# A memset that signals the change of rows, and a maximum at the start of the next step, in an attention and gated dense kernel

## The chip, the cores and the metric

One NeuronCore of one Trainium2 chip runs the whole kernel. The metric is the time of one execution on the device in microseconds (us); smaller is better. A profiled execution gives, beside its time, a trace of every instruction with start, duration and what released it. In its rows PE is TensorE (PEld its weight loads), ACT is ScalarE, DVE is VectorE, POOL is GpSimd and SP is SyncE, which issues the transfers.

## The reference

`x` has 2048 rows of 512 numbers. They are normalised, and two branches work on the result: attention with 32 heads of 16 columns that share one key and one value head, and two dense layers with 1792 hidden columns and a Mish between them. The gated product is added to `x`.

```python
def _A_ref(x, wq, wk, wv, wo):                    # H = 32, Dh = 16
    q = (x @ wq).reshape(B, S, H, Dh).transpose(0, 2, 1, 3)
    k, v = x @ wk, x @ wv
    scores = jnp.einsum("bhqd,bkd->bhqk", q, k) * (Dh ** -0.5)
    p = _softmax(scores, axis=-1)
    o = jnp.einsum("bhqk,bkd->bhqd", p, v)
    return o.transpose(0, 2, 1, 3).reshape(B, S, H * Dh) @ wo

def _B_ref(x, w1, b1, w2):
    h = jnp.einsum("bsd,df->bsf", x, w1) + b1
    sp = jnp.log1p(jnp.exp(-jnp.abs(h))) + jnp.where(h > 0, h, jnp.zeros_like(h))
    return jnp.einsum("bsf,fd->bsd", h * jnp.tanh(sp), w2)

xn = _layernorm(x, axis=-1)
return x + _A_ref(xn, wq, wk, wv, wo) * _silu(_B_ref(xn, w1, b1, w2))
```

## The kernel before

The attention is cut into 32 units (`NU`): four heads and 512 query rows each. A unit has 16 steps, one for each 128 of the 2048 key rows, so there are 512 steps (`NS`), in one order that the Python code writes out by hand: nothing reorders instructions afterwards, and every engine works through its own queue in the order in which the code issues. A lead of some 75 us loads `x`, normalises it and makes keys and values; then 492 steps run in the form that the change touches; the last 20 (`LEAD`) have a form of their own (`late_pair`).

Four kinds of products fill TensorE's queue in a step:

- **e** (`e_one`, tile `e`): keys times queries, four per step, each on 64 of the 128 rows of the array. ScalarE takes the exponential of each (tile `pt`). There are three banks for e.
- **m** (`m_one`, tile `m`): scores laid out the other way round, for the maximum of each query row of a later unit, on 64 rows, about four per step. VectorE reduces each to its maximum (tile `mb`, line L1131). There are three banks for m, and `m_one` is called a "maximum" below. The maxima are needed to shift the scores before the exponential; four small operations on VectorE per unit turn them, and transfers bring them into the query tile.
- **xps** (L120): the dense products: queries, both dense layers and the output projection. Every dense weight and input is split in two parts, high and low, and each dense product is cut into two halves of 64 rows. A *group* sums 12 or 15 dense products into the only bank `xps`.
- **pv** (`pv`, L1196): exponentials times values, on all 128 rows, in blocks of eight or sixteen records.

A product on rows 0 to 63 and one on rows 64 to 127 run at the same time. The function `waves` makes a step of this. In a step all dense products lie on one row half, `h = s % 2`; the four e and most of the maxima lie on the other half, and some maxima on the dense products' own half. In its code `xs` are the dense products, `a` the products of the other half, `b` the maxima of the own half. The loop takes in turn one of `xs` and one of `a`; when `xs` is empty, it takes `b` and the last of `a`.

A group of 12 runs in four steps of six dense products: six on one half (step 0 below, `gstep` 0), the same six on the other half (step 1), then the other six in the same way (steps 2 and 3). A group of 15 runs as 8, 8, 7, 7, the last ones with exceptions. In step 1 the block of pv stands in the middle (`mid`), behind steps 2 and 3 it stands at the end; step 0 and step 1 end without a block.

Both row halves add to the same bank, and they may not do it at the same time. So the first dense product of a step waits until the last dense product of the step before is done. It does so through a *relay*: an instruction on another engine that itself waits for TensorE beyond that product. Before the change the relay is the first instruction that follows on `a` when `xs` is empty, which in most steps is the exponential of an e:

```python
            if len(a) > 1 or a and not xs:
                r = a.popleft()()
                if k and not xs and relay is None:
                    relay = r
```

The last stage (`lane_part`, L638) already uses a memset of one column of the tile `turns` on VectorE as its relay; no maxima are left there.

Of the kernel before, what the change touches and what calls it, by code (L numbers as in the profile page):

```python
# [126 lines left out]
def block_kernel(ctx: ExitStack, tc: tile.TileContext, x, wq, wk, wv, wo, w1, b1, w2, out):  # L127
# [10 lines left out]
    pe, act, dve, pool, sp = nc.tensor, nc.scalar, nc.vector, nc.gpsimd, nc.sync  # L138

    step = [-10 ** 6]  # L140
    lead = {}
# [411 lines left out]
    def begin():  # L553
        prepare()
        if qqueue and is_ready(qqueue[0]):
            g = qqueue.popleft()
        elif queue and is_ready(queue[0]):
            g = queue.popleft()
        else:
            n = next((n for n, g in enumerate(queue) if g.wo is None), None)  # L560
            if not n or not is_ready(queue[n]) or queue[n].m1 is None:
                return False
            g = queue[n]
            del queue[n]
        if g.start:
            g.start()
        if len(g.mms) == 15 and spare_steps() > 1:
            g.most = 5
        if g.alloc:
            ps = g.alloc()  # L570
        else:
            ps = ps_x.tile([P, 512], F32, tag="x", name="xps")
        cur.update(g=g, n=0, ps=ps, chunk=[], relay=None)
        return True

    def finish():
        g = cur["g"]
        if cur["n"] < len(g.mms):
            return False
        for i in g.items:  # L580
            i.users -= 1
        cur["g"] = None
        evacs[0] += g.dve
        if lead:
            lead["post"](g, cur["ps"])
        else:
            g.post(cur["ps"])
            g.done = step[0]
        return True
# [17 lines left out]
    SYNC = mybir.DependencyInfo(mybir.DependencyClass.Sync, mybir.DependencyReason.DATA)  # L607
    turns = cp.tile([P, 2], F32, name="turns")
# [79 lines left out]
    def chunk_size(n, most):  # L688
        return -(-n // -(-n // most)) if n else 0

    gstep = [0]

    def waves(h, em, new, mid):

        if not cur["chunk"] and (not new or cur["g"] is None and not begin()):
            mms = []
        else:  # L700
            g = cur["g"]
            mms = cur["chunk"] or g.mms[cur["n"]:cur["n"] + chunk_size(len(g.mms) - cur["n"], g.most)]
        second = bool(cur["chunk"])
        k = len(mms)
        gstep[0] = 0 if not k or not second and cur["n"] == 0 else gstep[0] + 1
        if gstep[0] % 3 != 1:
            mid = None
        ms = em(k, second)
        a = deque(ms[1 - h])
        b = deque(ms[h])  # L710
        ps = cur["ps"]
        ends = second and cur["n"] + k == len(cur["g"].mms)
        xs = deque(mms)
        swap = k % 2 and k > 5 and not second
        relay = None
        first = True
        done = False
        while a or b or xs:
            if xs:
                i = xs.popleft().half(ps, h)  # L720
                if first and cur["relay"] is not None:
                    tc.add_manual_dep(i.ins, cur["relay"].ins.name, mybir.DependencyInfo(
                        mybir.DependencyClass.Sync, mybir.DependencyReason.DATA), reason="other half of the bank")
                first = False
                if ends and cur["g"].dve and len(xs) == HOLD + k % 2:
                    held[0] = []
                if not xs and ends:
                    cur["n"] += k
                    cur["chunk"] = []
                    finish()  # L730
                    done = True
                    for top in held[0] or ():
                        top()
                    held[0] = None
            elif b and not swap:
                b.popleft()()
# [4 lines that stand above are left out]
            if b and swap and not xs and not a:  # L741
                b.popleft()()
            if mid and len(xs) <= k // 2:
                mid()
                mid = None
        if k and not done:
            assert relay is not None
            cur["relay"] = relay
            if second:
                cur["n"] += k  # L750
                cur["chunk"] = []
            else:
                cur["chunk"] = mms
# [621 lines left out]
    for c0, c1 in ((0, 1), (1, 2), (2, 3), (3, 4)):  # L1375
# [4 lines left out]
        for c in range(c0, c1):  # L1380
            xs, scs = [], []
# [71 lines left out]
    def best(eng):  # L1453
        found = None
        for k in plan[eng]:
            s = k.start(T[eng])
            if s is not None:
                rank = max(s, T[eng] + 0.1) + WAIT_US * k.prio
                if found is None or rank < found[2]:
                    found = (s, k, rank)  # L1460
        return found
# [5 lines left out]
    while True:  # L1467
# [7 lines left out]
        b = best("PE")  # L1475
# [96 lines left out]
    for s in range(NS + 2000):  # L1572
        inm = s < NS - LEAD
        if inm or cur["chunk"]:
# [4 lines left out]
            def em(k, second):  # L1579
                n, rest = m_sides(1 - h, k, second) if inm else (0, 0)  # L1580
                x = deque(lambda i=i: e_one(s, i) for i in range(4))
                y = deque(lambda: m_one(1 - h) for _ in range(n))
                r = [[], []]
                for op in EM if k % 2 == 0 or k == 5 or second else EM[::-1]:
                    if op == "M" and y:
                        r[1 - h].append(y.popleft())
                    elif op == "E":
                        r[1 - h].append(x.popleft())
                r[h] = [lambda j=j: m_one(h, n + rest > 4 and j == rest - 1) for j in range(rest)]
                return r  # L1590
# [3 lines left out]
            def mid():  # L1594
                act_jobs(1 + (len(jobs) > 3))
                pv_halves(2 * s - 3)

            waves(h, em, s < NS - LEAD - 1, mid)
            if gstep[0] % 3 == 2 or cur["g"] is None or s == NS - LEAD - 1:
                act_jobs(1 + (len(jobs) > 3))  # L1600
# [59 lines left out]
```

## Time and profile before

| what | value |
|---|---|
| median of three runs | 1766.49 us (1766.31 to 1766.54) |
| the profiled execution, its own time | 1766.74 us |
| span of its trace | 1765.0 us |
| granted TensorE clock | 0.998 |
| TensorE busy | 1610.1 us |
| VectorE busy | 1351.9 us |
| ScalarE busy | 1313.9 us |

The span runs from the first to the last instruction of the trace; the 1.7 us around it belong to the execution's own time. A row of the timeline has the start and the duration in us, the engine, the line, the operation, what it writes and reads, and how many like it follow each other; in brackets stands how long the engine was idle before, and what ended that. TensorE's ends are modelled, and its products overlap. A row of the waits has who waited for whom, the total in us, how often, and the longest. A row of groups has the busy time in us, the mean of one in ns, and the idle time ahead of it. The lines themselves are shown with the prediction.

### The profile page before, as it was taken

What the parts mean: (1) busy time and instruction counts of PE and PEld (TensorE: products, weight loads), DVE (VectorE), ACT (ScalarE), POOL (GpSimd) and SP (SyncE); (2) the same over time, 40 slices, a digit from 0 to 9 for tenths busy, and PEclk for the clock granted to TensorE, in tenths of its full rate; (3) what the DMA queues carried; (4) which work ended last, traced back from release to release, by engine and by line L of the source; (5) the groups of instructions that cost most, each with busy time, mean ns of one, the idle gap of its engine ahead of it and who ended that gap; (6) DMA issues with size and microseconds to landing.
All of it is one profiled execution on the core that took longest, in us unless ns stands there. A gap on an engine that the chain in (4) does not pass through costs nothing.

```text
span 1765.0 us, 33610 instructions
## 1 busy us (share of the span) xinstructions
PE 1610.1 (91%) x12571; PEld 885.7 (50%) x12571; DVE 1351.9 (77%) x2332; ACT 1313.9 (74%) x2517; POOL 635.0 (36%) x683
## 2 busy tenths in 40 slices
PE   9998998999999899889999998999899999999997
PEld 5544544554544555445455545545555555555454
DVE  7987787788878778777887877777878888778722
ACT  7676777678877667767878776777678777768885
POOL 4772346263454104502322421145033231402541
PEclk9999999999999999999999999999999999999999
DMA  6231321141422213121103131220222312112020
GB/s 205 82 115 57 100 70 45 55 131 28 131 62 58 86 39 112 40 76 50 38 21 108 47 105 40 82 73 22 64 88 64 100 48 85 33 52 88 19 79 25
DMA packets 74674, 124.44 MB, mean 71 GB/s; under 512 B 21520, under 2 KB 35344, under 8 KB 74512
## 3 DMA queue, kind: packets, MB, share of 16 engines
q1 hardware_dynamic: 74512, 122.29, 22.7%
q8 instruction: 100, 1.64, 0.4%
q14 instruction: 62, 0.51, 0.1%
HBM read 74.78 MB, written 26.21 MB: 57 GB/s over the span
## 4 chain that ended last, share of the span: by engine, by line
PE 72%; ACT 21%; DVE 3%; issue 2%; DMA 1%; POOL 0%; SPq 0%; ACTq 0%; POOLq 0%; DVEq 0%
PE xps L120 33%; PE pv L1196 27%; ACT pt L1108 20%; PE m L1127 5%; PE e L1106 5%; DVE mb L1131 3%; PE late L120 1%; PE xps L116 0%; ACT os L1205 0%; PE late L1106 0%; DMA xin<-in_dram 0%; PE xp L302 0%; PE kp L351 0%; POOL y L164 0%; DMA qt<-cr 0%
## 5 line engine op out<-in xcount | busy, mean ns | idle before, releaser
L1131 DVE TENSOR_REDUCE mb<-m 128x1 f32<-128x512 f32 x2048 | 1285.0, 684 | 337.9 <-PE m L1127 295.7
L1108 ACT ACTIVATE pt<-e 128x512 f32<-128x512 f32 x2016 | 1066.8, 603 | 377.8 <-PE e L1106 343.4
L1127 PE MATMUL m<-ks,qt 48*128 48x512 f32 (+1 forms) x2048 | 828.3, 424 | 7.0 <-DVE mb L1131 6.1
L1106 PE MATMUL e<-qt,ks 64*128 64x512 f32 x2016 | 756.2, 411 | 1.5 <-DMA qt<-cr 1.2
L1196 PE MATMUL pv<-pt,vaug 128*32 128x512 f32 (+1 forms) x4968 | 519.2, 525 | 0.0
L1127 PEld LDWEIGHTS m<-ks,qt 48*128 48x128 f32 (+1 forms) x2048 | 370.7, 185 | 74.5 <-DVE mb L1131 41.1
L120 PE MATMUL xps<-wbs,act 64*128 64x512 f32 x1188 | 333.0, 410 | 56.7 <-ACT pt L1108 56.7
L1106 PEld LDWEIGHTS e<-qt,ks 64*128 64x128 f32 x2016 | 370.9, 186 | 19.5 <-ACT pt L1108 7.3
L120 PE MATMUL xps<-xt,ws 64*128 64x512 f32 x1104 | 317.3, 413 | 43.7 <-ACT pt L1108 43.3
L120 PEld LDWEIGHTS xps<-wbs,act 64*128 64x128 f32 x1188 | 203.8, 185 | 203.1 <-ACT pt L1108 97.7
L120 PEld LDWEIGHTS xps<-xt,ws 64*128 64x128 f32 x1104 | 187.1, 185 | 196.0 <-ACT pt L1108 116.3
L1196 PEld LDWEIGHTS pv<-pt,vaug 128*32 128x32 f32 x4968 | 122.3, 108 | 206.4 <-issue 178.8
L164 POOL TENSOR_TENSOR hb<-hb,t 128x512 f32<-128x512 f32 x56 | 72.1, 1287 | 220.2 <-ACT t L859 176.0
L174 POOL TENSOR_SCALAR t<-t 128x512 f32<-128x512 f32 x56 | 34.5, 615 | 320.2 <-ACT t L846 320.1
L120 PE MATMUL xps<-xt,wq 64*128 64x512 f32 x336 | 96.7, 414 | 14.3 <-ACT pt L1108 14.3
L120 PE MATMUL xps<-wbs,ot_all 64*128 64x512 f32 x288 | 82.7, 413 | 11.5 <-ACT pt L1108 11.5
L120 PEld LDWEIGHTS xps<-xt,wq 64*128 64x128 f32 x336 | 57.0, 185 | 61.2 <-ACT pt L1108 37.0
L120 PEld LDWEIGHTS xps<-wbs,ot_all 64*128 64x128 f32 x288 | 48.6, 184 | 51.3 <-ACT pt L1108 32.2
L164 POOL TENSOR_TENSOR hb<-hb,u 128x512 f32<-128x512 f32 x56 | 72.2, 1288 | 4.4
L164 POOL TENSOR_TENSOR u<-u,t 128x512 f32<-128x512 f32 x56 | 71.7, 1280 | 4.7
L164 POOL TENSOR_TENSOR act<-hb,act 128x512 fp32r<-128x512 f32 x55 | 70.9, 1288 | 4.6
L164 POOL TENSOR_TENSOR oc<-oc,sc 128x512 f32<-128x512 f32 (+1 forms) x16 | 20.7, 1291 | 125.6 <-ACT sc L1224 98.9
(162 smaller groups left out, 950.1 us busy)
## 6 DMA issues: line engine op xcount, KB each, us to landing
wbs<-w SPq DMA_DIRECT2D x36, 512.0 KB
ws<-w SPq DMA_DIRECT2D x35, 512.0 KB
qt<-qh SPq DMA_DIRECT2D x256, 32.0 KB
w<-wbs SPq DMA_DIRECT2D x14, 512.0 KB
wq<-wq SPq DMA_DIRECT2D x14, 512.0 KB
wbs<-wo SPq DMA_DIRECT2D x12, 512.0 KB
rawws<-in_dram SPq DMA_DIRECT2D x21, 256.0 KB
rawwb<-in_dram SPq DMA_DIRECT2D x20, 256.0 KB
```

The source lines that it names most:

```text
L120: i = self.pe.matmul(ps, self.lhs()[o], self.rhs()[o], start=(self.k == 0 and self.halves == 0), stop=(self.k == self.tot - 1 and self.hal ...
L164: eng.tensor_tensor(out=o, in0=a, in1=b, op=op)
L174: pool.tensor_scalar(o, o, lim, 0.0, op0=ALU.min, op1=ALU.max)
L1106: pe.matmul(e, ks[o:o + 64, P * k:P * (k + 1)], q[o:o + 64, p], start=True, stop=True)
L1108: r = act.activation(pt, e, AF.Exp, scale=0.25)
L1127: pe.matmul(m, q[o, p, P * t:P * (t + 1)], ks[o, C * kb:C * (kb + 1)], start=True, stop=True)
L1131: r = dve.reduce_max(out=mb_of[v][:, kb, z:z + 1], in_=m, axis=AX.X)
L1196: pe.matmul(o[32 * j:32 * j + 32, z], vaug[:, k], pt[:, z], start=(k == 0), stop=(k == 15))
```

## The change

```diff
@@ waves @@
         relay = None
         first = True
         done = False
+        own = gstep[0] % 3 > 0
         while a or b or xs:
-            if xs:
+            if own and b:
+                b.popleft()()
+                own = False
+            elif xs:
                 i = xs.popleft().half(ps, h)
                 if first and cur["relay"] is not None:
                     tc.add_manual_dep(i.ins, cur["relay"].ins.name, ...)
                 first = False
+                if not xs and not ends and not lead and gstep[0] % 3 < 2:
+                    relay = dve.memset(turns[:, 0:1], 0.0)
+                    tc.add_manual_dep(relay.ins, i.ins.name, SYNC, reason="half of the bank")
```

Two things are done, and what is computed stays the same. First, in steps 0 and 1 of a group (and 3 and 4 of the few with six steps) a memset of one column on VectorE is issued behind the last dense product and waits for it; it is the relay in the place of the exponential. There are 238 of them. Second, in steps 1 and 2 (4 and 5) the loop begins with one maximum of `b`, if there is one, and with the first of `a`, and only then takes the first dense product. A step of eight dense products has no maxima in `b`.

This is TensorE's queue at the end of step 0 and the start of step 1 of the group of twelve whose times the prediction reads (`m_0_` and `m_1_` are maxima on rows 0 to 63 and 64 to 127, `e_` the products for the exponentials; `waits` names the engines waited for). Before:

```order
L120 MATMUL xps<-xt_3778,ws_9290 128x512
L1106 MATMUL e_2_9686<-qt_79,ks 128x512 [waits Activation_49]
L1127 MATMUL m_1_7_9690<-ks,qt_78 128x512 [waits DVE_49]
L1106 MATMUL e_3_9693<-qt_79,ks 128x512 [waits Activation_49]
L120 MATMUL xps<-xt_3778,ws_9290 128x512 [waits Activation_49]
L1127 MATMUL m_1_8_9700<-ks,qt_78 128x512 [waits DVE_49]
```

And with the change:

```order
L120 MATMUL xps<-xt_3809,ws_9380 128x512
L1113 MATMUL e_2_9781<-qt_79,ks 128x512 [waits Activation_49]
L1134 MATMUL m_1_7_9785<-ks,qt_78 128x512 [waits DVE_49]
L1113 MATMUL e_3_9788<-qt_79,ks 128x512 [waits Activation_49]
L1134 MATMUL m_0_8_9794<-ks,qt_78 128x512 [waits DVE_49]
L1134 MATMUL m_1_8_9797<-ks,qt_78 128x512 [waits DVE_49]
L120 MATMUL xps<-xt_3809,ws_9380 128x512 [waits DVE_49]
```

Two maxima have moved ahead of step 1's first dense product, the own half's `m_0_8` and the other half's `m_1_8`, and that product waits for VectorE instead of ScalarE.

VectorE's queue over steps 0 and 1 of the same group: the reductions (`mb`) of the maxima named above. Before:

```order
L1131 TENSOR_REDUCE mb_9511<-m_0_5_9664 128x1 [waits PE_49]
L1131 TENSOR_REDUCE mb_9511<-m_0_6_9673 128x1 [waits PE_49]
L1131 TENSOR_REDUCE mb_9511<-m_0_7_9682 128x1 [waits PE_49]
L1131 TENSOR_REDUCE mb_9511<-m_1_7_9690 128x1 [waits PE_49]
L1131 TENSOR_REDUCE mb_9511<-m_1_8_9700 128x1 [waits PE_49]
L1131 TENSOR_REDUCE mb_9511<-m_1_9_9709 128x1 [waits PE_49]
L1131 TENSOR_REDUCE mb_9511<-m_1_10_9733 128x1 [waits PE_49]
L1131 TENSOR_REDUCE mb_9511<-m_0_8_9741 128x1 [waits PE_49]
```

And with the change:

```order
L1138 TENSOR_REDUCE mb_9603<-m_0_5_9758 128x1 [waits PE_49]
L1138 TENSOR_REDUCE mb_9603<-m_0_6_9767 128x1 [waits PE_49]
L1138 TENSOR_REDUCE mb_9603<-m_0_7_9776 128x1 [waits PE_49]
L730 MEMSET turns 128x1 [waits PE_49]
L1138 TENSOR_REDUCE mb_9603<-m_1_7_9785 128x1 [waits PE_49]
L1138 TENSOR_REDUCE mb_9603<-m_0_8_9794 128x1 [waits PE_49]
L1138 TENSOR_REDUCE mb_9603<-m_1_8_9797 128x1 [waits PE_49]
L1138 TENSOR_REDUCE mb_9603<-m_1_9_9806 128x1 [waits PE_49]
L1138 TENSOR_REDUCE mb_9603<-m_1_10_9830 128x1 [waits PE_49]
L730 MEMSET turns 128x1 [waits DVE_49,PE_49]
```

The first memset stands behind three reductions, the second behind eight in all; `m_0_8` has moved from the end of step 1 to its start.

TensorE's queue at the end of step 1 and the start of step 2. Before:

```order
L120 MATMUL xps<-xt_3778,ws_9290 128x512
L1106 MATMUL e_2_9737<-qt_77,ks 128x512 [waits Activation_49]
L1127 MATMUL m_0_8_9741<-ks,qt_78 128x512 [waits DVE_49]
L1106 MATMUL e_3_9744<-qt_77,ks 128x512 [waits Activation_49]
L120 MATMUL xps<-xt_3778,ws_9290 128x512 [waits Activation_49]
L1127 MATMUL m_0_9_9749<-ks,qt_78 128x512 [waits DVE_49]
```

And with the change:

```order
L1113 MATMUL e_2_9834<-qt_77,ks 128x512 [waits Activation_49]
L120 MATMUL xps<-xt_3809,ws_9380 128x512
L1113 MATMUL e_3_9840<-qt_77,ks 128x512 [waits Activation_49]
L1134 MATMUL m_1_11_9844<-ks,qt_78 128x512 [waits DVE_49]
L1134 MATMUL m_0_9_9847<-ks,qt_78 128x512 [waits DVE_49]
L120 MATMUL xps<-xt_3809,ws_9380 128x512 [waits DVE_49]
```

The last `e_2` stands one dense product earlier, and the two maxima of step 2's start stand between step 1's last product and step 2's first dense one.

## The prediction

> **What bounds the kernel now.** I read the page first: the busy shares and the chain that ended last.
>
> ```profile
> span 1765.0 us, 33610 instructions
> PE 1610.1 (91%) x12571; PEld 885.7 (50%) x12571; DVE 1351.9 (77%) x2332; ACT 1313.9 (74%) x2517; POOL 635.0 (36%) x683
> PE 72%; ACT 21%; DVE 3%; issue 2%; DMA 1%; POOL 0%; SPq 0%; ACTq 0%; POOLq 0%; DVEq 0%
> ```
>
> TensorE carries 72% of the chain and ScalarE 21%. So TensorE sets the pace, and now and then it waits for ScalarE. The list of waits says where:
>
> ```profile
> PE xps L120 <- ACT pt L1108: 130.8, 236, 0.9
> PEld m L1127 <- DVE mb L1131: 41.1, 85, 0.9
> ```
>
> 236 times a dense product (L120, tile xps) waits for an exponential (L1108), 0.55 us each: 130.8 us in all, nearly all of TensorE's idle time. 236 is two per group: these are the step ends inside a group where no block of pv products follows. The change works at exactly these places. Next I took the timeline of one usual group of twelve products; its four steps start at 701.28, 703.75, 707.75 and 711.11.
>
> ```profile
> 701.28 0.50 PE L120 MATMUL xps<-xt,ws 64*128 64x512 f32 x1
> 702.55 0.39 PE L120 MATMUL xps<-xt,ws 64*128 64x512 f32 x1
> 702.78 0.39 PE L1127 MATMUL m<-ks,qt 48*128 48x512 f32 x1
> 703.75 0.50 PE L120 MATMUL xps<-xt,ws 64*128 64x512 f32 x1 [0.48 <-ACT pt L1108]
> 704.32 0.39 PE L120 MATMUL xps<-xt,ws 64*128 64x512 f32 x1
> 704.63 1.50 PE L1196 MATMUL pv<-pt,vaug 128*32 128x512 f32 x16
> 706.06 0.50 PE L120 MATMUL xps<-xt,ws 64*128 64x512 f32 x1
> 707.75 0.49 PE L120 MATMUL xps<-xt,ws 64*128 64x512 f32 x1 [0.48 <-ACT pt L1108]
> 709.25 0.40 PE L1127 MATMUL m<-ks,qt 48*128 48x512 f32 x1
> 709.68 1.50 PE L1196 MATMUL pv<-pt,vaug 128*32 128x256 f32 x16
> 711.11 0.50 PE L120 MATMUL xps<-xt,ws 64*128 64x512 f32 x1
> ```
>
> A dense product and a product on the other row half run as a pair; pairs follow each other every 0.23 us (702.55 to 702.78), the first one after a wait or a block takes 0.34. The six dense products of step 0 have all started by 702.55, but the next step's first starts at 703.75. On the other engines at that time:
>
> ```profile
> 702.12 2.06 ACT L1108 ACTIVATE pt<-e 128x512 f32<-128x512 f32 x4 [0.35 <-PE e L1106]
> 706.61 1.58 ACT L1108 ACTIVATE pt<-e 128x512 f32<-128x512 f32 x3 [0.88 <-PE e L1106]
> 701.85 3.76 DVE L1131 TENSOR_REDUCE mb<-m 128x1 f32<-128x512 f32 x6 [0.42 <-PE m L1127]
> 706.87 1.29 DVE L1131 TENSOR_REDUCE mb<-m 128x1 f32<-128x512 f32 x2 [1.26 <-PE xps L120]
> L1131 DVE TENSOR_REDUCE mb<-m 128x1 f32<-128x512 f32 x2048 | 1285.0, 684 | 337.9 <-PE m L1127 295.7
> ```
>
> The signal used now is the third exponential of the row from 702.12. But VectorE is not free either: six reductions run back to back from 701.85. One takes 0.684 us and six take 3.76, so they follow each other every (3.76 - 0.684)/5 = 0.615. The third, whose maximum stands ahead of the last dense product, ends at 701.85 + 0.684 + 2 x 0.615 = 703.76: the very moment at which the wait on ScalarE ends. This is the row that decides: **the new signal stands behind a queue as long as the old one's.**
>
> **The change, first half: the signal.** The memset itself is shown by the last stage, which already uses one:
>
> ```profile
> L638 DVE MEMSET turns<- 128x1 f32 x40 | 2.1, 59 | 43.9 <-PE late L120 22.1 <-PE xps L120 21.5 <-PE e L1106 0.3
> 1718.59 0.09 DVE L638 MEMSET turns<- 128x1 f32 x2 [2.18 <-PE xps L120]
> 1718.74 0.18 PEld L120 LDWEIGHTS late<-xt,act 64*128 64x128 f32 x1 [0.19 <-DVE turns L638]
> ```
>
> It takes 0.06 us, and TensorE wakes 0.06 after it (1718.68 to 1718.74). Two memsets need 0.09 together, so a follower on VectorE may start a little before its forerunner ends; I add the full 0.06 behind the reduction. The bounds of the signal are then -0.01 us (it starts 0.07 early, as reductions do: 0.684 against 0.615) and +0.19 us (the whole wait of the last row, added to the reduction's end); I take 0.12, the sum of the two measured pieces. The Trainium skill, "VectorE: DVE Perf Modes", section "The DRAIN you can't avoid", says that the next operation starts only once the pipe is empty. By it the signal is 0.12 behind the reduction; by the reductions' spacing in this trace, 0.07 less, which over 2 x 88 boundaries would be 12 us to the good.
>
> So step 1 would start at 703.76 + 0.12 = 703.88 instead of 703.75: **+0.13 us**. Nothing is won by the signal alone here. The 238 memsets take 14 us of VectorE, covered by its idle 337.9 us. What queues behind each are reductions, and for those TensorE's next maxima wait, through their banks; no DMA and no queue of SyncE or GpSimd is moved past.
>
> **Second half: the maximum first.** In step 1 and step 2 of a group of twelve, the maximum of the dense products' own half and the first product of the other half now stand ahead of the signal; the pair at each step's end goes. Step by step, for the group shown:
>
> - Step 1 up to its pv block. There are three banks for maxima. The first product of the other half is a maximum too and needs the bank that the third reduction frees (703.76), so it cannot go ahead of the signal by much; in the trace this is so already (85 waits, 41.1 us). Of the pair, only the own maximum goes into the gap. Since the other half's list has moved up by one, four of its products, not three, stand ahead of the block: +0.23. One more maximum stands in the queue, so the second maximum of the list waits for a bank until the reduction behind the memset ends, 703.82 + 0.615 + 0.06 = 704.50, which is 0.62 after the step's start where 0.57 was free: +0.05. Together **+0.28**; unhidden, since TensorE takes its queue in order.
> - From the block's end to step 2. Before: 706.06 to 707.75 = 1.69. The last maximum ahead of the signal is now in the first pair behind the block, one pair earlier. Its reduction starts 0.57 after that pair (701.28 to 701.85), takes 0.684, then 0.12: 1.37. **-0.32**. This holds if VectorE has caught up by then; five reductions from 703.82 on, less the last, end at 706.3, the last one's start is due at about 703.88 + 2.59 + 0.57 = 707.04. Both products for step 2's start find free banks, so the pair is wholly in the gap.
> - Step 2. It had 707.75 to 711.11 = 3.36, with seven pairs; six are left. -0.23 for the pair. The block started 0.43 after the last pair (709.25 to 709.68), but 0.31 behind a pair with a dense product in step 1 (704.32 to 704.63), which the last pair now is: another -0.12 at most. I take **-0.30**. The signal of this step's end is still an exponential, now the fourth, not the third: four take 2.06, and with the first due at about 0.57 after the step's start it ends at 2.63, under the 3.06 that the step needs. Covered by the pv block of 1.43; without that block it would stop TensorE.
>
> Sum for a group of twelve: 0.13 + 0.28 - 0.32 - 0.30 = **-0.21 us** of about 12.74. By the program's order 88 groups run as 6, 6, 6, 6: -18.5 us.
>
> The 28 groups of fifteen run as 8, 8, 7, 7. With eight products a step keeps no maximum of its own, so step 1 starts as before; only step 2 does begin with one.
>
> ```profile
> 608.29 0.49 PE L120 MATMUL xps<-wbs,act 64*128 64x512 f32 x1
> 608.85 2.48 DVE L1131 TENSOR_REDUCE mb<-m 128x1 f32<-128x512 f32 x4 [1.06 <-PE m L1127]
> 611.24 0.50 PE L120 MATMUL xps<-wbs,act 64*128 64x512 f32 x1 [0.82 <-ACT pt L1108]
> 614.36 1.29 DVE L1131 TENSOR_REDUCE mb<-m 128x1 f32<-128x512 f32 x2 [1.27 <-PE m L1127]
> 615.77 0.49 PE L120 MATMUL xps<-wbs,act 64*128 64x512 f32 x1 [0.77 <-ACT pt L1108]
> ```
>
> Four reductions from 608.85 end at 611.33; with 0.12 the signal is at 611.45, against 611.24: +0.21. At the second boundary the reductions end at 615.65, with 0.12 exactly at the old 615.77: 0. Step 2 sheds a pair: -0.30. Sum -0.09, times 28: -2.5 us. The few other groups are left at nothing, and the last stage is not touched.
>
> In all -18.5 - 2.5 = -21 us. The profiled execution took 1766.74 us around its span of 1765.0; less 21 that is 1745.7, and against the median of 1766.49 **1745.5 us**, 1.2% less. By the terms' bounds a group of twelve may come out between 0.00 + 0.23 - 0.39 - 0.35 = -0.51 (no wait for the bank, early signal) and +0.20 + 0.35 - 0.25 - 0.23 = +0.07: -45 to +6 us, and the groups of fifteen add some -6 to +2. The terms won't all sit at one end, so the likeliest case's own range is 1730 to 1758.
>
> **Rivals.**
>
> *The wait goes altogether.* If VectorE were free at the boundaries, each of the 236 waits of 0.55 would shrink to the 0.19 that a bare memset costs in the last stage: 236 x 0.36 = 85 us, 1681 us. Idle time of VectorE is there, 337.9 us ahead of the reductions; but it lies behind the pv blocks (1.26 us ahead of 706.87), not at the first boundary, where the row of six has no gap. Chance 0.02.
>
> *Nothing moves.* The two shed pairs are worth 0.46 a group. If the bank waits in step 1 cost 0.26 and not 0.05, because two maxima, not one, meet a taken bank, the group stands at zero: 1766 us. For it: every maximum in step 1 is one bank nearer to its reduction. Against: behind the first, reductions come every 0.615 and maxima every 0.46 for two at most, then the block gives 1.43. Chance 0.10.
>
> *Slower: one more reduction ahead of the second memset.* VectorE enters step 1 with three reductions behind the memset where it had two. If it has not caught up when the last maximum comes, the signal into step 2 slips by one reduction, 0.615 us. One slip eats the gain of three groups; from 34 of the 88 groups on (21/0.615) the change loses. With two groups in three slipping, -21 + 59 x 0.615 = +15: 1782 us. For it: small reductions for the row shift and additions of y also run on VectorE between them, and the waits of reductions for maxima show that it is never far from full in steps 0 and 1. Against: 0.7 us of slack, worked out above. Chance 0.18.
>
> **How the numbers follow.** The forecast has 0.70, the rivals 0.02, 0.10 and 0.18. A measurement of this kernel can tell 0.2%, 3.5 us, from no change. The forecast and the first rival are faster: 0.72; nothing moves: 0.10; slower: 0.18. The range takes in the likeliest case's own, a little of the terms' lower ends, and upwards nothing moves and the slower rival up to some 58 slipped groups: 1728 to 1779 us.
>
> **What would show it.** Right: the waits of xps for pt fall from 236 to some thirty or fewer, and waits of xps for turns stand in their place, short ones in groups of twelve (0.1 to 0.3 us), near 0.9 in step 0 of groups of fifteen; the waits of m for mb grow well over 41.1 us; steps 0 and 1 of a group of twelve take about 2.60 and 3.96 us, step 2 3.06, the group 12.5. Wrong: a reduction between the last maximum of step 1 and its memset still running from before (the slower rival), an exponential as the releaser of step 3's first product, or waits of m for mb that take more than 0.3 us at the third product of step 1.

## The result, and the profile after

| | before | with the change |
|---|---|---|
| median | 1766.51 us (1766.31 to 1766.99, 4 runs) | 1743.12 us (1742.38 to 1743.23, 4 runs) |
| ratio | | 0.9866, 95% interval 0.9849 to 0.9883 |
| span of the profiled execution | 1765.0 us | 1741.2 us |

The change makes the kernel faster by 23.4 us; 21 had been forecast. The page of the changed kernel, with the span, the busy shares and the chain that ended last by engine:

```profile
span 1741.2 us, 33855 instructions
PE 1668.2 (96%) x12571; PEld 894.3 (51%) x12571; DVE 1345.7 (77%) x2570; ACT 1327.5 (76%) x2517; POOL 634.0 (36%) x683
...
PE 75%; DVE 19%; issue 3%; ACT 1%; POOL 1%; DMA 0%; SPq 0%; POOLq 0%; DVEq 0%; ACTq 0%
```

ScalarE's 21% of the chain have become VectorE's 19%: the wait has not gone, it has changed hands. TensorE's busy share rose from 91% to 96%, which says less than it seems, since the work is the same 12571 records: products that used to run beside another one now run by themselves in the gap. Added up over the trace, exactly one product (pv apart) was at work, and no pv, for 69 us before and for 132 us with the change. The list of waits (who for whom, us in total, how often, the longest):

```profile
PEld m L1134 <- DVE mb L1138: 94.4, 263, 0.9
PEld xps L120 <- DVE turns L730: 89.3, 135, 1.5
PEld m L1134 <- DVE turns L730: 35.9, 89, 0.4
PE xps L120 <- DVE turns L730: 25.1, 27, 1.1
PE xps L120 <- ACT pt L1115: 1.1, 1, 1.1
```

Of 236 waits of a dense product for an exponential one is left. 27 waits for the memset, 0.93 us each on average, have come; 25 of them stand at the first step end of groups of fifteen, two at the second of groups of twelve. In the other groups of twelve the same wait no longer shows as idle time of TensorE, only of its weight loads, because the early maxima fill it. And maxima wait more than twice as long for banks (94.4 us against 41.1).

The same group of twelve as in the prediction, from the timeline, TensorE and then VectorE (start, length, engine, line, operation); its steps start at 692.88, 695.41, 699.43 and 702.65, the next group at 705.56:

```profile
694.39 1.50 PE L1134 MATMUL m<-ks,qt 48*128 48x512 f32 x3
695.41 0.49 PE L120 MATMUL xps<-xt,ws 64*128 64x512 f32 x1
695.73 0.39 PE L1113 MATMUL e<-qt,ks 64*128 64x512 f32 x1
...
696.00 0.49 PE L1134 MATMUL m<-ks,qt 48*128 48x512 f32 x1
...
696.34 0.40 PE L1113 MATMUL e<-qt,ks 64*128 64x512 f32 x1
696.66 1.50 PE L1203 MATMUL pv<-pt,vaug 128*32 128x512 f32 x16
698.09 0.50 PE L120 MATMUL xps<-xt,ws 64*128 64x512 f32 x1
...
699.43 0.50 PE L120 MATMUL xps<-xt,ws 64*128 64x512 f32 x1
699.64 0.47 PE L1113 MATMUL e<-qt,ks 64*128 64x512 f32 x1
...
700.89 0.41 PE L1113 MATMUL e<-qt,ks 64*128 64x512 f32 x1
701.22 1.50 PE L1203 MATMUL pv<-pt,vaug 128*32 128x256 f32 x16
702.65 0.50 PE L120 MATMUL xps<-xt,ws 64*128 64x512 f32 x1
```

```profile
693.45 2.50 DVE L1138 TENSOR_REDUCE mb<-m 128x1 f32<-128x512 f32 x4 [0.42 <-PE m L1134]
695.28 0.06 DVE L730 MEMSET turns<- 128x1 f32 x1
...
698.66 0.69 DVE L1138 TENSOR_REDUCE mb<-m 128x1 f32<-128x512 f32 x1 [0.92 <-PE xps L120]
699.30 0.06 DVE L730 MEMSET turns<- 128x1 f32 x1
```

And the weight loads of the two early maxima in the first gap (PEld):

```profile
694.79 0.18 PEld L1134 LDWEIGHTS m<-ks,qt 48*128 48x128 f32 x1 [0.24 <-DVE mb L1138]
695.39 0.18 PEld L1134 LDWEIGHTS m<-ks,qt 48*128 48x128 f32 x1 [0.42 <-DVE turns L730]
```

The first memset stands behind three reductions without a gap ahead of it. (The row of four takes in the fourth reduction, which stands behind the memset in the queue and runs beside it.) The step that it releases starts 2.53 us after the last one, not earlier than before (2.47). Of the two early maxima only the first, the own half's, goes into the gap. The second needs the bank of the third reduction, which ends at 695.34, in the same moment as the memset (to which the profile puts the wait down), and its weights load only 0.02 us ahead of the dense product's at 695.41. The second memset stands behind a single reduction that began 0.57 after the block of pv. The whole group takes 12.68 us against 12.74, and this is one of the poorer ones; over all groups the sums come below.

### The profile page after: what moved, and what is told of

It reads as the page before. It is cut to its first block, busy times and chain, and to the rows that moved or that the text cites. A ratio compares the mean times of both kernels' runs of the same rounds, so it can differ in the third digit from the quotient of the medians.

```text
span 1741.2 us, 33855 instructions
## 1 busy us (share of the span) xinstructions
PE 1668.2 (96%) x12571; PEld 894.3 (51%) x12571; DVE 1345.7 (77%) x2570; ACT 1327.5 (76%) x2517; POOL 634.0 (36%) x683
## 4 chain that ended last, share of the span: by engine, by line
PE 75%; DVE 19%; issue 3%; ACT 1%; POOL 1%; DMA 0%; SPq 0%; POOLq 0%; DVEq 0%; ACTq 0%
PE xps L120 28%; PE pv L1203 26%; DVE mb L1138 17%; PE m L1134 10%; PE e L1113 8%; PE xps L116 1%; DVE y L164 1%; PE late L120 1%; ACT pt L1115 0%; DVE y L920 0%; DVE turns L730 0%; DMA xin<-in_dram 0%; PE late L1113 0%; PE xp L302 0%; PE kp L351 0%
## 5 line engine op out<-in xcount | busy, mean ns | idle before, releaser
L1115 ACT ACTIVATE pt<-e 128x512 f32<-128x512 f32 x2016 | 1080.8, 603 | 340.1 <-PE e L1113 243.8
L1134 PEld LDWEIGHTS m<-ks,qt 48*128 48x128 f32 (+1 forms) x2048 | 355.0, 185 | 159.1 <-DVE mb L1138 94.4
L120 PE MATMUL xps<-xt,ws 64*128 64x512 f32 x1104 | 323.2, 418 | 5.8
L120 PEld LDWEIGHTS xps<-xt,wq 64*128 64x128 f32 x336 | 56.7, 185 | 43.3 <-ACT pt L1115 11.7
L120 PEld LDWEIGHTS xps<-wbs,ot_all 64*128 64x128 f32 x288 | 48.9, 184 | 36.7 <-ACT pt L1115 11.7
```

Source lines behind the costliest of these rows:

```text
L120: i = self.pe.matmul(ps, self.lhs()[o], self.rhs()[o], start=(self.k == 0 and self.halves == 0), stop=(self.k == self.tot - 1 and self.hal ...
L1115: r = act.activation(pt, e, AF.Exp, scale=0.25)
L1134: pe.matmul(m, q[o, p, P * t:P * (t + 1)], ks[o, C * kb:C * (kb + 1)], start=True, stop=True)
```

## The experiments

Ten kernels, e1 to e10, each timed over five rounds beside the kernel before (medians 1767.1 to 1767.3 us there).

**The signal alone (e1).** The memset stays, no maximum comes first:

```diff
-        own = gstep[0] % 3 > 0
+        own = False
```

> The memset stays, no step begins with a maximum. Theory (signal and early pair are worth something only together): the signal stands behind as long a queue on VectorE as on ScalarE; in a group of twelve +0.10 us at the first boundary, -0.10 at the second; in a group of fifteen +0.19 and 0. Time 1769 us, 1765 to 1774; the 236 waits of xps stay, now for turns. Rival (the signal is the gain): 1741 to 1755 us.

Measured: 1755.51 us, ratio 0.9933 (0.9919 to 0.9946). The theory's size was missed, and so was the rival's: half of the gain comes with the signal alone. I took the usual group's terms for all 88. Eight of the groups of twelve have only two maxima among the first step's dense products; the old signal is the fourth exponential there, and only two reductions stand ahead of the new one. Before, such a first step took 2.91 to 2.95 us, in e1 it takes 1.91 to 1.94 (first dense product to first dense product): 8 x 1.0 = 8 us. The 80 usual ones lose 8 at the first boundary, as expected, and all 88 win 9 at the second. The prediction had said of the first boundary that nothing is won by the signal alone: that holds for the usual groups, not for the kernel.

**The early maximum alone (e2).** The memset is gone, the exponential signals again:

```diff
-                if not xs and not ends and not lead and gstep[0] % 3 < 2:
+                if False:
```

> The steps begin with a maximum, the signal is the old one, an exponential. Theory: since the other half's list has moved up by one, the exponential that signals step 1's end is the fourth and not the third, 0.55 us later in its row; a group of twelve: +0.08 (bank at the first boundary) +0.27 (four products ahead of the block) +0.27 (later signal) -0.27 (shed pair) = +0.35 us, times 88; a group of fifteen -0.32, times 28. Time 1788 us, 1775 to 1800. Rival (the pair in the gap is the gain, whatever signals): 1741 to 1755 us.

Measured: 1795.34 us, ratio 1.0158 (1.0144 to 1.0172): slower than before, as the theory had it. ScalarE and TensorE at the second boundary of the same group:

```profile
720.93 1.09 ACT L1115 ACTIVATE pt<-e 128x512 f32<-128x512 f32 x2 [1.00 <-PE e L1113]
720.14 0.50 PE L120 MATMUL xps<-xt,ws 64*128 64x512 f32 x1
722.07 0.49 PE L120 MATMUL xps<-xt,ws 64*128 64x512 f32 x1 [0.74 <-ACT pt L1115]
```

From the block's end at 720.14 to step 2 it takes 1.93 us (1.69 before, 1.34 with the change): the signal is now the step's fourth exponential, the second of this row, 720.93 + 1.09 = 722.02. The theory holds term by term: over the 88 groups of twelve step 0 takes 6.8 us more than before, step 1 47.1 more and step 2 18.6 less, where 7, 48 and 24 were expected. So the two halves of the change don't add: -11.7 alone, +28.1 alone, -23.4 together.

**The early maximum without its partner (e3).** The own maximum comes first, but the first product of the other half stays behind the first dense one:

```diff
             if own and b:
                 b.popleft()()
                 own = False
+                continue
             elif xs:
```

> As the change, but the early maximum goes alone: the first product of the other half stays behind the first dense product. Theory (the gain comes from a whole pair that is shed, and the second signal's last maximum being one pair earlier): both are gone, since the other half still has seven products for six dense ones; group of twelve +0.10 +0.05 -0.11 -0.05 = 0, group of fifteen +0.1. Time 1768 us, 1761 to 1774. Rival (the early maximum in itself fills the gap): 1741 to 1752 us.

Measured: 1765.93 us, ratio 0.9994 (0.9985 to 1.0002): no difference that can be told from the kernel before. An early maximum in the gap is worth nothing as long as the other half still has seven products for six dense ones; against e1 it even loses ten.

**No memset in steps of eight (e4).** The place where the prediction had found a loss:

```diff
-                if not xs and not ends and not lead and gstep[0] % 3 < 2:
+                if not xs and not ends and not lead and gstep[0] % 3 < 2 and k < 8:
```

> As the change, but steps of eight dense products keep the exponential as their signal. Theory: the first boundary of most groups of fifteen gets back the 0.19 us that four reductions ahead of the memset cost (25 x 0.19 = 4.8), three of the groups lose the 0.6 that the memset gave them, the second boundary stays as it is: 1740 us, 1737 to 1743. Rival (the memset helps in every step): 1746 us or more.

Measured: 1740.58 us, ratio 0.9851 (0.9837 to 0.9864), as the theory had it, though its interval overlaps the change's own. The traces tell the two apart: step 0 of all groups of fifteen takes 82.3 us, as before the change, and 85.1 with it. VectorE and TensorE at that place in the changed kernel (this group starts at 601.25):

```profile
601.82 2.48 DVE L1138 TENSOR_REDUCE mb<-m 128x1 f32<-128x512 f32 x4 [1.06 <-PE m L1134]
604.25 0.06 DVE L730 MEMSET turns<- 128x1 f32 x1
604.38 0.50 PE L120 MATMUL xps<-wbs,act 64*128 64x512 f32 x1 [1.00 <-DVE turns L730]
```

The next step starts after 3.13 us, where the exponential had let it start after 2.95.

**The memset ahead of the last reduction (e5).** If the queue ahead of the signal is what costs, it should stand one reduction further ahead. For groups of fifteen, first step only; the reduction is held until the memset has been issued:

```diff
-                if not xs and not ends and not lead and gstep[0] % 3 < 2:
+                if not xs and not ends and not lead and (k < 8 and gstep[0] % 3 < 2 or k == 8 and gstep[0] % 3 == 0):
                     relay = dve.memset(turns[:, 0:1], 0.0)
                     ...
+                    for top in held[0] or ():
+                        top()
+                    held[0] = None
...
+            if xs and len(xs) < 3 and not ends and not lead and k == 8 and gstep[0] % 3 == 0:
+                held[0] = held[0] or []
```

> As e4, but in the first step of a group of fifteen the memset is issued ahead of the last reduction instead of behind it. Theory (the length of the signal's queue is what costs there): the memset follows the third reduction, 2.48 us after the step's start, and the next step starts at 2.60 instead of 2.95: 25 x 0.35 = 9 us less than e4's 1740.6, 1732 us, 1727 to 1737. Rival (the banks of the next step hold it anyway): 1740 us, as e4.

Measured: 1728.63 us, ratio 0.9779 (0.9766 to 0.9793), 12 us less than e4. In the same group (start 598.26):

```profile
600.66 0.06 DVE L730 MEMSET turns<- 128x1 f32 x1
600.79 0.49 PE L120 MATMUL xps<-wbs,act 64*128 64x512 f32 x1 [0.40 <-DVE turns L730]
```

The step starts after 2.53 us, not 2.60 as expected, and TensorE's wait there falls from 1.00 to 0.40. In the traces the 25 usual groups give 10.3 us at this place. Another 1.8 come from the three groups of fifteen with only two maxima, which get back the memset that e4 had taken from them; the expectation had left them out.

**Four more memsets (e6).** The signal's price, by making it longer:

```diff
-                    relay = dve.memset(turns[:, 0:1], 0.0)
-                    tc.add_manual_dep(relay.ins, i.ins.name, SYNC, reason="half of the bank")
+                    for _ in range(5):
+                        relay = dve.memset(turns[:, 0:1], 0.0)
+                        tc.add_manual_dep(relay.ins, i.ins.name, SYNC, reason="half of the bank")
```

> The change with four more memsets behind each one, the last of the five being the signal. Theory (the signal's end sets when the next step's dense products start, at all 234 boundaries): each boundary moves by the four memsets' time, 0.24 us at 0.06 each, more if each waits for the one ahead: 56 us or more on top of 1743, 1795 to 1850. Rival (the bank of the first maximum holds the start, the signal has slack): 1743 to 1755 us.

Measured: 1862.69 us, ratio 1.0542 (1.0524 to 1.056). The five write the same column, so each waits for the one ahead:

```profile
741.93 0.45 DVE L731 MEMSET turns<- 128x1 f32 x4
742.45 0.06 DVE L731 MEMSET turns<- 128x1 f32 x1
```

Five start within 0.52 us, 0.13 apart. Against the change (e7) the kernel is 120.3 us longer; 238 signals x 4 x 0.13 = 124. Step by step in the two traces, the 232 steps that end with a signal in groups of twelve and of fifteen take 0.50 us more on average, and none less than 0.25 more. What is put ahead of the signal is paid at every boundary: there is no slack behind it.

**The change again (e7)**, for comparisons:

> The change itself, for comparison on the same chip: 1743 us, 1740 to 1746, by every theory.

1742.37 us, ratio 0.9857 (0.9844 to 0.9871).

**An exponential's product first in step 1 (e8).** The maximum that can't go into the gap for want of a bank changes places with a product that can:

```diff
+                early = k == 6 and rest and gstep[0] % 3 == 1
-                for op in EM if k % 2 == 0 or k == 5 or second else EM[::-1]:
+                for op in "EMEMMEEM" if early else EM if k % 2 == 0 or k == 5 or second else EM[::-1]:
```

> The change, but in step 1 of a group of twelve the other half's list begins with a product for an exponential, and the maxima follow second, fourth and fifth. Theory (at the first boundary the pair doesn't fit into the gap because its maximum waits for the third reduction's bank): now the whole pair fits, the block of pv comes after three pairs again, the last maximum stays in the first pair behind the block: 0.28 us per group of twelve, 88 x 0.28 = 25 us less, 1718 us, 1708 to 1728. Rival (VectorE's queue sets the pace of step 1, in whatever order): 1738 to 1746 us.

Measured: 1723.08 us, ratio 0.9748 (0.9734 to 0.9761), 19.3 us less than the change; 25 were expected. TensorE in step 1 of the same group:

```profile
687.23 0.46 PE L1113 MATMUL e<-qt,ks 64*128 64x512 f32 x1
687.64 0.49 PE L120 MATMUL xps<-xt,ws 64*128 64x512 f32 x1
687.98 0.39 PE L120 MATMUL xps<-xt,ws 64*128 64x512 f32 x1
688.23 0.50 PE L1134 MATMUL m<-ks,qt 48*128 48x512 f32 x1
688.65 1.50 PE L1203 MATMUL pv<-pt,vaug 128*32 128x512 f32 x16
```

The product for the exponential has started at 687.23, inside the gap. The block starts 1.01 us after the step's first dense product, where it started after 1.25 with the change. Step 1 gets shorter by 0.22 to 0.25 us in each of the 80 usual groups, and by 17.4 in all 88; another 2.2 come from step 0 of groups with only two maxima. VectorE's queue is as long as before, so it is the bank of the first maximum that had kept the pair out.

**Both improvements (e9), and one more (e10).** e9 has the edits of e5 and e8; e10 also holds the last reduction behind the memset in the first step of groups of twelve (`k in (6, 8)`).

> e5 and e8 together: no memset behind four reductions in groups of fifteen but one ahead of the last, and the exponential's product first in step 1 of groups of twelve. They act on different groups, so the gains add: 1742.4 - 13.7 - 19.3 = 1709 us, 1705 to 1714, by every theory; 1720 or more would say that another engine has become the bound.

> e9, and the memset ahead of the last reduction in the first step of groups of twelve too. Theory (at that boundary the signal and the third reduction's bank are due together, so an earlier signal only moves the wait to the next maximum, whose bank comes 0.06 us later than now): no gain, 0 to +0.1 us per group of twelve, 1709 to 1718 us. Rival (the length of the signal's queue is all that counts): the signal comes some 0.5 us earlier in 88 groups, 1665 to 1690 us.

Measured: e9 1709.11 us, ratio 0.9671 (0.9657 to 0.9685); e10 1709.02 us, 0.9672 (0.9659 to 0.9686). e9 comes out as expected, and is faster than the kernel before and than the change. e10 gets its signal earlier and gains nothing by it:

```profile
681.73 0.06 DVE L730 MEMSET turns<- 128x1 f32 x1
682.17 0.39 PE L120 MATMUL xps<-xt,ws 64*128 64x512 f32 x1
682.45 0.50 PE L1139 MATMUL m<-ks,qt 48*128 48x512 f32 x1
683.47 0.64 PE L1208 MATMUL pv<-pt,vaug 128*32 128x512 f32 x4
```

This group starts at 679.92. Its second step starts after 2.25 us instead of 2.53, but the next maximum in the queue stands at 682.45, 2.53 after the group's start: it waits for the bank that the held reduction frees. Summed over the 88 groups, step 0 takes 22.6 us less than in e8 and step 1 takes 22.4 more.

## Why the prediction was right

For the check I added up, over all groups in both traces, the time from each step's first dense product to the next step's (changes from the sums before rounding).

| steps, us in all | before | predicted change | after | measured change |
|---|---|---|---|---|
| 88 groups of twelve: step 0 | 220.8 | +11.4 | 224.1 | +3.3 |
| step 1 | 358.5 | -3.5 | 356.5 | -2.0 |
| step 2 | 292.3 | -26.4 | 273.0 | -19.2 |
| step 3 | 305.6 | 0 | 305.5 | -0.1 |
| 28 groups of fifteen: step 0 | 82.3 | +5.9 | 85.1 | +2.8 |
| step 1 | 127.1 | 0 | 127.0 | -0.1 |
| step 2 | 100.8 | -8.4 | 91.7 | -9.1 |
| step 3 | 87.2 | 0 | 86.0 | -1.3 |

The groups gave 25.6 us by this table, the rest of the kernel gave back 1.8 (the spans differ by 23.8). The mechanism is the one that was forecast: the signal changes hands and gains nothing in the usual group at the first boundary, step 1 loses ahead of its block about what it wins behind it, and the pair is shed in step 2. That the total came out so close is in part luck: step 0 of the groups of twelve was forecast 8.1 us too long and step 2 7.2 too short, and these errors nearly cancel. Point by point:

- *The new signal stands behind a queue as long as the old one's.* Right for the usual group: its first memset comes behind three reductions, and the step starts after 2.53, not earlier. e6 shows that a longer queue is paid at every boundary; a shorter one is not always a gain, as e10 shows. Too general all the same: the eight groups of twelve and three of fifteen with only two maxima there win up to 1.0 and 0.6 us by the signal. (In these three a step of eight does have two maxima on its own half.) With the whole change four of the eight keep it (1.93 to 1.94 us), four get back 0.15 only (2.76 to 2.80): there two maxima stand ahead of step 1's first dense product, and the second one's weight load waits some 0.7 us for a reduction (0.70 at 169.34). Where the gain is kept, step 1 has no maximum of its own half to begin with. The 80 usual groups lost 7.8 us and the eight won 4.5, so step 0 lost 3.3, not 11.4. For the whole kernel the signal alone does win: 11.7 us in e1, 9 of them at the second boundary of the groups of twelve.
- *The signal's own 0.12 us.* 0.08 measured: the memset starts at 695.28 and ends at 695.34, and the step follows at 695.41, 0.08 behind the end of the third reduction (before rounding). At the second boundary the memset starts 0.05 ahead of the reduction's end (699.30 against 698.66 + 0.69 = 699.35). The Trainium skill, "VectorE: DVE Perf Modes", section "The DRAIN you can't avoid", has the next operation wait until the pipe is empty, and says that one that is not held starts earlier. The early start agrees with the exception, which the prediction left out.
- *Step 1 up to the block, +0.28.* Right in its cause, too small: 698.09 - 695.41 = 2.68 against 2.31, +0.37. The maximum stands at 0.59 and not at 0.57, a small wait, but the pair behind it then takes 0.34 instead of 0.23, as the first pair of a step does. Here the price of a stop is the wait plus 0.11.
- *From the block to step 2, -0.32.* Right: 1.34, forecast 1.37. VectorE had been idle for 0.92 us ahead of that reduction, so the slower rival's condition, one more reduction in the queue, was not met. Nor was it in any of the 88 groups: VectorE had been idle for 0.5 us or more ahead of that reduction in each.
- *Step 2, -0.30.* A little large: (292.3 - 273.0)/88 = 0.22, and 0.14 in the group shown. The part that I had doubted is there, since the block follows the last pair after 0.33 us (700.89 to 701.22). In the group shown the first product for an exponential stands 0.21 behind its dense partner (699.64), which takes back a part; which wait holds it there was not tried.
- *Groups of fifteen, -0.09 each.* The boundaries are right (3.13 forecast as 3.16, and 0 at the second), step 2 as well (-0.32). The three groups with two maxima bring the first boundary down to +2.8, and step 3 gives 1.3 that was not forecast and stays unexplained. In all these groups gave 7.6 us, where 2.5 had been forecast.
- *The signs.* Those of being right came, but the group shown takes 12.68 us where 12.5 was named, and the short waits of the groups of twelve show on the weight loads only. One sign of being wrong stands there by its letter: the weight load of step 3's first product waits for an exponential (0.84 us at 702.65). It did so before as well (0.84 at 711.11), and step 3 starts 1.43 us behind the block's start both times, so nothing is lost by it.
- *Two slips of reckoning.* The 130.8 us of waits are 84% of TensorE's idle time (1765.0 - 1610.1 = 154.9), and the range's upper end, 1779, stands for 54 slipped groups ((1779 - 1745.5)/0.615), not 58. Neither moves the forecast.

That the two halves depend on each other, which no term of the prediction said, is the clearest thing the runs showed: the early maximum without the memset costs 28.1 us, and with it the change gains 11.7 more than the memset alone. e2 gives the reason: moving the other half's list up makes the old signal one exponential later, and the memset takes the signal off that list. e3 gives the other: without the move, no pair is shed, and an early maximum gains nothing. That the wait would go altogether is refuted by the 89.3 us that the weight loads still wait for the memset; that nothing moves, by the time; the slower rival, by the time and by VectorE's idle time ahead of the second memset.

## What to carry to other kernels

A signal from an in-order engine costs what stands in the queue ahead of it, not its own 0.06 us: count the instructions ahead, and issue the signal ahead of the last one that it doesn't need (10 us here, on 25 boundaries). It pays only where the signal comes last: in groups of twelve the same step gained nothing, since the next product waited for the very reduction that had been moved behind the signal. Before moving work into a wait, ask what each moved piece itself waits for: a product that needed a bank stayed outside the gap, one that needed none went in and was worth 19 us. And where two edits depend on each other, one alone can be slower than neither.

## What was unexpected of the hardware

Behind a stop of TensorE of only 0.02 us between paired products, the next pair comes after 0.34 us instead of 0.23 (696.00 to 696.34), so 0.02 us of waiting cost 0.13. It is not this group alone: in 83 of the 88 groups of twelve the third pair of step 1 comes 0.25 or 0.26 us behind the second, and the next product 0.33 or 0.34 behind that. A memset on VectorE overlaps the reduction ahead of it (0.05 us) and the one behind, but memsets that wait for one another stand 0.13 apart, more than twice their length; two with different columns took 0.09 together in the last stage before the change.
